# Three chunks of attention ahead of the first MoE, weight pieces spread over 44 units, and z turned in 32x32 squares on VectorE, in a fused attention and two-MoE kernel

## Chip, cores and metric

One core of a Trainium2 chip. The metric is the device time of one execution in microseconds. Three runs of the kernel before gave 5212.89, 5213.58 and 5214.27 us; the median, 5213.58 us, is the time before.

## What is computed

Eight sequences of 3072 tokens pass through attention with a squared ReLU, a gated MLP ("the first MoE") and a mixture of eight experts with one expert a token ("the second MoE"). Cut to what matters:

```python
scores = (1.0 / S) * np.matmul(z, z.transpose(0, 2, 1))      # z: 8 x 3072 x 64
x = u * np.matmul(np.maximum(scores, 0.0) ** 2, v)           # u, v: 8 x 3072 x 256
xn = x / np.sqrt(np.mean(x * x, -1, keepdims=True) + 1e-06) * rms_g
g = xn @ w_gate                                              # 256 x 1536, float64 in memory
x = (g / (1 + np.exp(-g)) * (xn @ w_val)) @ w_out
e_idx, keep = np.argmax(x @ moe2_w_gate, 1), x @ moe2_w_skip > 0
out = x + keep * prob[e_idx] * (np.maximum(x @ w1[e_idx], 0) @ w2[e_idx])
```

## The kernel before

The 24,576 tokens are 48 chunks of 512 (`CH`), six to a sequence. An attention phase of one chunk ("a") and a first-MoE phase of one chunk ("m") have 12 units each. Each fp32 operand is split into a rounded high part and the remainder (`split`, L221 to L228), and one product is three matmuls (`mm3`, L230 to L233). So an attention unit has 4 score matmuls (L566, L567) and 12 on v (L231 to L233), and a MoE unit 12 on gate and value weights and 6 on the output weights, all over 512 columns.

The order is written out by hand. `Stream.unit` issues a unit's front (scores, ReLU and square on ScalarE, the splits on ScalarE, VectorE and GpSimd), and two units later its back, the product that needs the splits (`LAG = 2`). `st.later(d, fn)` puts other steps in front of the unit d units on; every engine's queue, SyncE's DMA issues among them, runs strictly in that order. The phases stand as a0 a1 m0 a2 m1 a3 ... a47 m46 m47, then the second MoE.

Beside the first phases, the first MoE's weights are prepared in 18 pieces (`w_prep`, unit numbers in the table `w_at`). They arrive as float64, and each piece is decoded in three VectorE instructions (`high`, L358 to L360), three more and an addition on GpSimd (`low`, L363 to L371), and split on ScalarE and GpSimd (`parts`, L375, L376). A piece's room is loaded again (`w_next`) when `low` is done with it. In the same stretch eight DMAs of 1325 KB fill the expert buffer with pads (`pad_prep`, L209), one a unit, and `row_prep` (L194 to L198) loads the router's rows.

z is loaded in rows, split on VectorE (`z_split`), put side by side as high and low, turned on TensorE by four 128x128 transposes a chunk (`z_turn`, L269), and copied by ScalarE (L273). For sequence 0 that happens at the start; for the others in the last attention phase before and the MoE phase after it (`batch_prep`).

After a phase come the chunk's tails: attention's product with u and its norm, either through TensorE transposes (`attn_turn`, `xn_turn`, chunks 0, 1 and 47) or in 32x32 squares on VectorE (`in_blocks`), and the MoE's router. The router takes dot products on VectorE (L654) from a copy through memory, or, for the last `QUICK = 2` chunks, transposes (L406) and small matmuls (L637) on TensorE.

Of the kernel before, what the change touches and what calls it, by code (L numbers as in the profile page):

```python
# [20 lines left out]
P = 128  # L21
# [49 lines left out]
def tile_relu2_attention_moe_moe2(  # L71
# [68 lines left out]
    stage = {}  # L140
    for q, tag in ((0, "acct"), (1, "u")):
        g0, g1 = 4 * q, min(NCB, 4 * q + 4)
        if g0 < g1:
            t = sp.tile([P, g1 - g0, KT, DQ], F32, tag=tag, name=f"z0_{q}", bufs=1)
            for g in range(g0, g1):
                nc.sync.dma_start(
                    t[:, g - g0], z[0, g * CH : (g + 1) * CH, :].rearrange("(k p) d -> p k d", k=KT)
                )
                stage["z", 0, g] = t[:, g - g0]

# [63 lines left out]

    st = Stream()
    QUICK = 2
    W_LOW, W_PARTS = 1, 3
    XNT, RS = 3, 2
# [35 lines left out]
    def z_load(b, g):  # L254
        t = sp.tile([P, KT, DQ], F32, tag="z2", name=f"zn_{b}_{g}", bufs=2)
        nc.sync.dma_start(t, z[b, g * CH : (g + 1) * CH, :].rearrange("(k p) d -> p k d", k=KT))
        stage["z", b, g] = t

    def z_split(b, g):
        t = stage.pop(("z", b, g))  # L260
        cat = sp.tile([P, KT, 2, DQ], F32R, tag="zcat", name=f"zc_{b}_{g}", bufs=1)
        split(cat[:, :, 0, :], cat[:, :, 1, :], t)
        stage["zc", b, g] = cat

    def z_turn(b, g):
        cat = stage.pop(("zc", b, g))
        ps = side(f"zps_{b}_{g}")
        for k in range(KT):
            nc.tensor.transpose(  # L269
                ps.bitcast(F32R)[:, 0, k * P : (k + 1) * P], cat[:, k, :, :].rearrange("p a d -> p (a d)"), identr  # L270
            )
# [11 lines left out]
    def v_load(b, g):  # L283
        t = sp.tile([P, KT, D], F32, tag="x" if b == 0 and g % 2 else "stage", name=f"vn_{b}_{g}", bufs=1)
        nc.sync.dma_start(t, v[b, g * CH : (g + 1) * CH, :].rearrange("(k p) d -> p k d", k=KT))
        stage["v", b, g] = t
# [9 lines left out]
    WIDE = moe_w_gate.dtype != F32  # L296
    pieces = [(kind, q, h) for q in range(FQ) for kind in "gv" for h in range(DH)]
    GV = len(pieces)
    pieces += [("o", q, h) for q in range(FQ) for h in range(DH)]

# [8 lines left out]
    def w_room(i):  # L309

        if i < GV:
            return i % 4
        return 0 if i == GV else 4

    def w_load(i):
        kind, q, h = pieces[i]
        w = {"g": moe_w_gate, "v": moe_w_val, "o": moe_w_out}[kind]
        src = w_piece(w, kind, q, h)
        room, n = w_room(i), src.shape[2]
        if room % 4 == 0:  # L320
            tag = "stage" if room else "xn"
            t = sp.tile([P, 2, n], U32 if WIDE else F32, tag=tag, name=f"wst_{i}", bufs=1)
        else:
            t = wraw[:, room - 1, : 2 * n].rearrange("p (o f) -> p o f", o=2)
            t = t if WIDE else t.bitcast(F32)
        nc.sync.dma_start(t, src)
        stage["w", i] = t
# [7 lines left out]
    def w_prep(i):  # L335
# [3 lines left out]
        if kind == "o":  # L339
            f = q * KT + h * KT // 2  # L340
            if i == GV:
                new_wo()
# [6 lines left out]
        if WIDE:  # L349
            bits = t.rearrange("p o (f t) -> p (o f) t", t=2)  # L350
            lo, hi = bits[:, :, 0], bits[:, :, 1]
            flat = (wrb if i < GV and i % 4 > 1 else ytok).rearrange("p k w -> p (k w)")
            dst = flat[:, (i % 2) * CH : (i % 2 + 1) * CH]
# [8 lines left out]
        def low():  # L362
# [7 lines left out]
            )  # L370
            nc.gpsimd.tensor_add(dst, dst, hf)  # L371
            w_next(i)

        def parts():
            nc.scalar.copy(w[:, 0], t)  # L375
            nc.gpsimd.tensor_sub(w[:, 1], t, w[:, 0].bitcast(F32))  # L376
            if not WIDE:
                w_next(i)

        if WIDE:  # L380
            high()
# [48 lines left out]
    def x_blocks(ci, x):  # L430
# [7 lines left out]
        def times_u():  # L438
# [28 lines left out]
    def attn_turn(ci, acct):  # L467
# [61 lines left out]
    def xn_split(ci, t, xn, h):  # L529
# [5 lines left out]
        if h == DH - 1:  # L535
            XN[ci] = xn
            u_load(ci + 1)

    def xn_turn(ci, x):
# [8 lines left out]
        tag, bufs = ("vhl", 6) if ci == NCH - 1 else ("xn", 1)  # L548
        xn = sp.tile([P, 2, DH, CH], F32R, tag=tag, name=f"xn_{ci}", bufs=bufs)
# [3 lines left out]
    def attn_phase(ci):  # L553
# [291 lines left out]
    class Group:  # L845
# [84 lines left out]
        def tail1(self, t, yt):  # L930
# [146 lines left out]
    st.later(2 * NCB - 2, lambda: w_load(GV + 1))  # L1077
    for i, n in enumerate(w_at):
# [3 lines left out]
    for ci in range(NCH):  # L1082
        order.append(("a", ci))
        if ci >= 1:
            order.append(("m", ci - 1))
    order.append(("m", NCH - 1))

    for i, (kind, ci) in enumerate(order):
# [6 lines left out]
        if kind == "a":  # L1095
            if (ci + 1) % NCB == 0 and ci + 1 < NCH:
# [82 lines left out]
```

## Time and profile before

| | |
|---|---|
| median of three runs | 5213.58 us |
| profiled execution, and its span | 5214.61 us, 5212.8 us |
| TensorE (PE) busy | 5132.3 us, 98% |
| VectorE (DVE) busy | 3576.1 us, 69% |
| ScalarE (ACT) busy | 2705.3 us, 52% |
| GpSimd (POOL) busy | 427.3 us, 8% |
| granted TensorE clock, mean | 0.995 |

The span runs from the first to the last instruction; 1.8 us of the execution lie around it. A busy PE is a PE with a matmul in flight: matmuls overlap, so the number of matmuls in a stretch tells more than its busy time.

### The profile page before, as it was taken

What the parts mean: (1) busy time and instruction counts of PE and PEld (TensorE: products, weight loads), DVE (VectorE), ACT (ScalarE), POOL (GpSimd) and SP (SyncE); (2) the same over time, 40 slices, a digit from 0 to 9 for tenths busy, and PEclk for the clock granted to TensorE, in tenths of its full rate; (3) what the DMA queues carried; (4) which work ended last, traced back from release to release, by engine and by line L of the source; (5) the groups of instructions that cost most, each with busy time, mean ns of one, the idle gap of its engine ahead of it and who ended that gap; (6) DMA issues with size and microseconds to landing.
All of it is one profiled execution on the core that took longest, in us unless ns stands there. A gap on an engine that the chain in (4) does not pass through costs nothing. (4 is left out here: it accounts for less than half of the span.)

```text
span 5212.8 us, 65890 instructions
## 1 busy us (share of the span) xinstructions
PE 5132.3 (98%) x23724; PEld 4258.5 (82%) x23724; DVE 3576.1 (69%) x8966; ACT 2705.3 (52%) x3559; POOL 427.3 (8%) x428
## 2 busy tenths in 40 slices
PE   7899999999999999999999999999999999999998
PEld 5688888888888888888888888888888888888888
DVE  8667767677677776777767767777677767554446
ACT  6445545465465554655546546455465554433344
POOL 5100000000000000000000000000000000021111
PEclk9999999999999999999999999999999999999999
DMA  5201101021011110110102001111011110122225
GB/s 163 57 19 42 44 20 37 19 60 26 19 37 35 39 31 19 42 44 20 35 19 66 21 19 37 38 39 27 19 43 43 24 32 19 41 86 86 78 94 161
DMA packets 547841, 234.43 MB, mean 45 GB/s; under 512 B 422357, under 2 KB 528000, under 8 KB 547384
## 3 DMA queue, kind: packets, MB, share of 16 engines
q1 hardware_dynamic: 533496, 205.00, 16.0%
q0 software_dynamic: 14016, 25.21, 1.4%
q8 instruction: 186, 3.05, 0.3%
q14 instruction: 143, 1.17, 0.1%
HBM read 144.79 MB, written 99.30 MB: 47 GB/s over the span
## 5 line engine op out<-in xcount | busy, mean ns | idle before, releaser
L738 ACT ACTIVATE gr<-gv 128x512 f32<-128x512 f32 x576 | 345.9, 600 | 1166.7 <-PE gv L233 1166.7
L232 PE MATMUL acc<-a,v 128*128 128x512 f32 x2304 | 900.3, 391 | 12.7 <-DVE a L228 8.8
L231 PE MATMUL acc<-a,v 128*128 128x512 f32 x2304 | 899.1, 390 | 1.7 <-ACT acct L427 1.7
L233 PE MATMUL acc<-a,v 128*128 128x512 f32 x2304 | 898.9, 390 | 0.0
L228 DVE TENSOR_TENSOR a<-r,a 128x512 fp32r<-128x512 f32 x1128 | 738.5, 695 | 23.4 <-ACT a L227 4.0
L569 ACT ACTIVATE r<-s 128x1024 f32<-128x1024 f32 x576 | 591.3, 1027 | 296.8 <-PE s L567 278.2
L654 DVE CUSTOM_DVE_ANT_0 jk<-ytok,wrb 128x256 bf16<-128x256 f32 x1656 | 698.6, 422 | 35.2
L739 DVE TENSOR_TENSOR gr<-gr,gv 128x512 f32<-128x512 f32 x576 | 395.4, 686 | 442.9 <-ACT gr L738 439.1
L228 DVE TENSOR_TENSOR h<-gr,h 128x512 fp32r<-128x512 f32 x576 | 399.4, 693 | 395.8 <-ACT h L227 395.8
L227 ACT CAST h<-gr 128x512 fp32r<-128x512 f32 x576 | 357.9, 621 | 577.1 <-DVE gr L739 577.1
L570 ACT ACTIVATE r<-r 128x1024 f32<-128x1024 f32 x576 | 611.3, 1061 | 18.4
L703 POOL DMA_INDIRECT xs<-ytok,pu x192 | 210.2, 1095 | 4070.5 <-DVE pu L701 2871.0
L232 PEld LDWEIGHTS acc<-a,v 128*128 128x128 f32 x2304 | 434.0, 188 | 108.3 <-DVE a L228 11.9
L231 PEld LDWEIGHTS acc<-a,v 128*128 128x128 f32 x2304 | 434.4, 189 | 93.2 <-ACT acct L427 2.1
L233 PEld LDWEIGHTS acc<-a,v 128*128 128x128 f32 x2304 | 434.0, 188 | 90.0
L225 DVE CAST a<-r 128x512 fp32r<-128x512 f32 x564 | 237.5, 421 | 340.2 <-ACT r L570 340.0
L231 PE MATMUL gv<-xn,wg_s 128*128 128x512 f32 x1152 | 455.2, 395 | 13.7 <-DVE gr L739 13.6
L567 PE MATMUL s<-z,z 128*128 128x512 f32 x1152 | 452.4, 393 | 0.1
L232 PE MATMUL gv<-xn,wg_s 128*128 128x512 f32 x1152 | 449.4, 390 | 1.1 <-DVE xn L228 1.1
L233 PE MATMUL yacc<-h,wo_s 128*128 128x512 f32 x1152 | 449.4, 390 | 0.6 <-POOL wo_s L376 0.6
L231 PE MATMUL yacc<-h,wo_s 128*128 128x512 f32 x1152 | 449.3, 390 | 0.4 <-ACT wo_s L375 0.4
L232 PE MATMUL yacc<-h,wo_s 128*128 128x512 f32 x1152 | 449.0, 390 | 0.0
(200 smaller groups left out, 9034.4 us busy)
## 6 DMA issues: line engine op xcount, KB each, us to landing
raw<-in_moe_w_dram SPq DMA_DIRECT2D x76, 512.0 KB
vn<-in_v_dram SPq DMA_DIRECT2D x48, 512.0 KB
out_dram<-ytok SPq DMA_DIRECT2D x48, 512.0 KB
ys<-yb SPq DMA_DIRECT2D x368, 64.0 KB
ytok<-ys SPq DMA_DIRECT2D x46, 512.0 KB
u<-in_u_dram SPq DMA_DIRECT2D x360, 64.0 KB
xs<-pad SPq DMA_DIRECT2D x8, 1325.0 KB
xt<-xs SPq DMA_DIRECT2D x16, 530.0 KB
```

The source lines that it names most:

```text
L225: nc.vector.tensor_copy(hi, src)
L227: nc.scalar.copy(hi, src)
L228: (nc.vector if lo_eng == "v" else nc.gpsimd).tensor_sub(lo, src, hi.bitcast(F32))
L231: nc.tensor.matmul(ps, w_hi, x_hi, start=start, stop=False)
L232: nc.tensor.matmul(ps, w_hi, x_lo, start=False, stop=False)
L233: nc.tensor.matmul(ps, w_lo, x_hi, start=False, stop=stop)
L567: nc.tensor.matmul(ps[:, t], zj, zi2, start=False, stop=True)
L569: nc.scalar.activation(out=r, in_=ps, func=AF.Relu)
L570: nc.scalar.activation(out=r, in_=r, func=AF.Square)
L654: nc.vector.tensor_tensor_reduce(out=junk, in0=ytok[:, k, :D], in1=wrb[:, e, :], op0=ALU.mult, op1=ALU.add, scale=1.0, scalar=0.0, accum_o ...
L738: nc.scalar.activation(out=r[:, 0], in_=ps[:, 0], func=AF.Silu)
L739: nc.vector.tensor_mul(r[:, 1], r[:, 0], ps[:, 1])
```

## The change

The new order is a0 a1 a2 m0 a3 m1 ... a47 m45 m46 m47 (`LEAD = 2`), with two x tiles instead of one. The weight pieces go over units 3 to 43 (before: 2 to 33) in another order, with other rooms; their addition and their last subtraction move from GpSimd to VectorE, as does the low part of the second half of a score tile (`split`'s "g"). Pads are asked for every fourth unit from unit 14 (before: every unit from 16), `row_prep` at unit 49 (before: 24). z is loaded in 32-token by 32-feature squares, twice (so that both halves of the partitions hold the features), turned by one VectorE transpose, and split there; PE and ACT take no part in it. `QUICK` is 3.

```diff
+    def z_in(t, b, g):
+        blocks = z[b, g * CH : (g + 1) * CH, :].rearrange("(b c) (q r) -> q c b r", c=Q, r=Q)
+        for q in range(4):
+            nc.sync.dma_start(t[q * Q : (q + 1) * Q].rearrange("p (b r) -> p b r", r=Q), blocks[q % 2])
+        stage["z", b, g] = t
...
-            st.later(first + e, fill)
+            st.later(first + 4 * e, fill)
...
-    QUICK = 2
-    W_LOW, W_PARTS = 1, 3
+    LEAD = 2
+    QUICK = 3
+    W_LOW, W_PARTS = 1, 2
...
     def z_split(b, g):
-        t = stage.pop(("z", b, g))
-        cat = sp.tile([P, KT, 2, DQ], F32R, tag="zcat", name=f"zc_{b}_{g}", bufs=1)
-        split(cat[:, :, 0, :], cat[:, :, 1, :], t)
+        t = sp.tile([P, CH], F32, tag="zcat", name=f"zt_{b}_{g}", bufs=1)
+        nc.vector.transpose(t, stage.pop(("z", b, g)))
...
     def z_turn(b, g):
-        for k in range(KT):
-            nc.tensor.transpose(
-                ps.bitcast(F32R)[:, 0, k * P : (k + 1) * P], cat[:, k, :, :].rearrange("p a d -> p (a d)"), identr
-            )
         z1 = sp.tile([P, CH], F32R, tag="z1", name=f"z1_{b}_{g}", bufs=NCB)
-        nc.scalar.copy(z1, ps[:, 0, :])
+        nc.vector.tensor_copy(z1, t)
+        nc.vector.tensor_sub(z1[DQ:, :], t[DQ:, :], z1.bitcast(F32)[DQ:, :])
...
-            nc.gpsimd.tensor_add(dst, dst, hf)
+            nc.vector.tensor_add(dst, dst, hf)
             w_next(i)
-        def parts():
+        def high_part():
             nc.scalar.copy(w[:, 0], t)
-            nc.gpsimd.tensor_sub(w[:, 1], t, w[:, 0].bitcast(F32))
+        def low_part():
+            nc.vector.tensor_sub(w[:, 1], t, w[:, 0].bitcast(F32))
...
-        return 2 <= ci < NCH - 1
+        return LEAD < ci < NCH - 1
...
-                    split(o[:, 0], o[:, 1], r[:, t], "a" if t == 1 or ci == 1 else "v", "g" if t == 1 and ci <= 1 else "v")
+                    split(o[:, 0], o[:, 1], r[:, t], "a" if t == 1 or (0 < ci <= LEAD and k % 2) else "v")
...
-    st.later(2 * UPC, row_prep)
-    pad_prep(4 * UPC // 3)
+    st.later(4 * UPC + 1, row_prep)
+    pad_prep(UPC + 2)
...
-    w_at = [2, 4, 6, 8, 10, 11, 13, 14, 15, 16, 18, 19, 20, 21, 24, 27, 30, 33]
+    w_at = [3, 7, 11, 13, 15, 18, 21, 24, 27, 29, 31, 33, 35, 37, 38, 39, 41, 43]
...
-        if ci >= 1:
-            order.append(("m", ci - 1))
-    order.append(("m", NCH - 1))
+        if ci >= LEAD:
+            order.append(("m", ci - LEAD))
+    order += [("m", ci) for ci in range(NCH - LEAD, NCH)]
```

The order on DVE in chunk 0, from the low step of the first weight piece to unit 6 (`wst` is the piece as loaded, `ytok` its decoding, `a` a split score tile, `zc` and `zt` z before it is turned and after). Before:

```order
L363 SCALAR_TENSOR_TENSOR ytok<-wst_168,ytok 128x512
L366 TENSOR_SCALAR wst_168<-ytok 128x512
L368 SCALAR_TENSOR_TENSOR wst_168<-wst_168 128x512
L225 CAST a_3_0_274<-r_3_271 128x512
L228 TENSOR_TENSOR a_3_0_274<-r_3_271,a_3_0_274 128x512
L225 CAST zc_3_292<-z_0_78 128x4x64
L228 TENSOR_TENSOR zc_3_292<-z_0_78,zc_3_292 128x4x64
```

And now:

```order
L376 SCALAR_TENSOR_TENSOR ytok<-wst_180,ytok 128x512
L379 TENSOR_SCALAR wst_180<-ytok 128x512
L381 SCALAR_TENSOR_TENSOR wst_180<-wst_180 128x512
L384 TENSOR_TENSOR ytok<-ytok,wst_180 128x512
L234 CAST a_4_0_305<-r_4_302 128x512
L237 TENSOR_TENSOR a_4_0_305<-r_4_302,a_4_0_305 128x512
L237 TENSOR_TENSOR a_4_1_308<-r_4_302,a_4_1_308 128x512
L276 CAST z_0_3_324<-zt_3_289 128x512
L277 TENSOR_TENSOR z_0_3_324<-zt_3_289,z_0_3_324 64x512
L237 TENSOR_TENSOR v_3_327<-vn_3_207,v_3_327 128x1024
```

The piece's addition, the second low part and z's split have joined DVE's queue; GpSimd's queue, which held such rows throughout these phases, holds none of them now.

The order on PE where a sequence begins, in its first attention phase. Before:

```order
L233 MATMUL acc_4578<-a_0_1_4617,v_0_4196 128x512
L269 MATMUL zps_4_4687<-ident,zc_4_4626 128x128 x4
L566 MATMUL s_3_4701<-z_1_0_4099,z_1_1_4260 128x512
L567 MATMUL s_3_4701<-z_1_0_4223,z_1_1_4260 128x512
L566 MATMUL s_3_4701<-z_1_0_4099,z_1_1_4260 128x512
```

And now:

```order
L242 MATMUL acc_4161<-a_0_1_4200,v_0_3787 128x512
L586 MATMUL s_3_4281<-z_1_0_3684,z_1_1_3846 128x512
L587 MATMUL s_3_4281<-z_1_0_3814,z_1_1_3846 128x512
L586 MATMUL s_3_4281<-z_1_0_3684,z_1_1_3846 128x512
L587 MATMUL s_3_4281<-z_1_0_3814,z_1_1_3846 128x512
```

The 48 rows of z transposes are gone from PE.

The order on SyncE (SP) around the pads (`wst`, `wraw` and, after the change, `wrb` are rooms of weight pieces; what an issue waits for stands behind it). Before:

```order
L326 DMA wst_758<-in_moe_w_out_dram 128x2x512 [waits DMAHW7_49,Pool_49]
L209 DMA xs<-pad 128x10x265 [waits DMAHW6_49]
L209 DMA xs<-pad 128x10x265
L209 DMA xs<-pad 128x10x265 [waits DMAHW0_49]
L209 DMA xs<-pad 128x10x265 [waits DMAHW1_49]
L209 DMA xs<-pad 128x10x265 [waits DMAHW2_49]
L209 DMA xs<-pad 128x10x265 [waits DMAHW3_49]
L326 DMA wst_999<-in_moe_w_out_dram 128x2x512 [waits DMAHW4_49,Pool_49]
```

And now:

```order
L339 DMA wrb<-in_moe_w_out_dram 128x2x512 [waits DMAHW4_49]
L216 DMA xs<-pad 128x10x265
L216 DMA xs<-pad 128x10x265 [waits DMAHW6_49]
L216 DMA xs<-pad 128x10x265 [waits DMAHW7_49]
L417 DMA u_1061<-in_u_dram 128x4x256 [waits DMAHW3_49,DMAHW0_49,DVE_49]
L339 DMA wst_1100<-in_moe_w_gate_dram 128x1024 [waits DMAHW1_49,DVE_49]
L216 DMA xs<-pad 128x10x265 [waits DMAHW2_49]
L339 DMA wst_1174<-in_moe_w_gate_dram 128x1024 [waits DVE_49]
```

Six pads stood in a row between two weight loads; now at most three do, and the rest stand one by one.

## Rows read from the trace of the kernel before

**Rows 1.** The page: busy time, share and instructions of each engine.

```profile
PE 5132.3 (98%) x23724; PEld 4258.5 (82%) x23724; DVE 3576.1 (69%) x8966; ACT 2705.3 (52%) x3559; POOL 427.3 (8%) x428
```

**Rows 2.** Windows: stretch, length, busy and count by engine, PE clock, DMA share, GB/s.

```profile
0.00:253.05 253.05, 202.43 (x825) 158.18 (x825) 191.92 (x310) 145.48 (x198) 92.17 (x81) 0.93 0.42 114
...
100.00:150.00 50.00, 38.23 (x150) 28.37 (x149) 43.93 (x63) 29.18 (x39) 30.58 (x21) 0.93 0.76 220
150.00:200.00 50.00, 36.23 (x151) 29.24 (x150) 23.91 (x43) 14.15 (x29) 7.49 (x6) 0.83 0.43 69
...
305.24:439.53 134.29, 134.22 (x592) 110.60 (x593) 97.07 (x256) 83.16 (x102) 8.60 (x10) 1.00 0.17 36
```

**Rows 3.** Timeline of PE: a unit of a0, the first of m1 (start us, us).

```profile
13.37 0.80 PE L566 MATMUL s<-z,z 128*128 128x512 f32 x1
...
253.05 0.39 PE L231 MATMUL gv<-xn,wg_s 128*128 128x512 f32 x1
```

**Rows 4.** Waits of PE, 0 to 253 us (total us, times, longest us).

```profile
PE gv L231 <- DVE gr L739: 13.6, 1, 13.6
PE zps L269 <- DVE zc L228: 13.4, 5, 3.9
```

**Rows 5.** Timeline: DVE beside GpSimd, then alone (in brackets: idle before).

```profile
17.00 1.62 POOL L228 TENSOR_TENSOR a<-r,a 128x512 fp32r<-128x512 f32 x1 [2.50 <-ACT a L227]
17.38 1.40 DVE L225 CAST zc<-z 128x256 fp32r<-128x256 f32 x1
...
175.29 0.43 DVE L358 TENSOR_SCALAR ytok<-wst 128x512 uint32<-128x512 uint32 x1 [17.24 <-DMA wst<-in_moe_w_out_dram]
175.75 0.43 DVE L359 TENSOR_SCALAR ytok<-ytok 128x512 f32<-128x512 f32 x1
```

**Rows 6.** Timeline of SP: the pads, the router's rows and a weight piece.

```profile
103.25 20.04 SPq L209 DMA_DIRECT2D xs<-pad  x6
...
147.81 6.55 SPq L197 DMA_DIRECT2D wsc<-in_moe_w_skip_dram  x1
167.28 0.35 SPq L198 DMA_DIRECT2D wrb<-wsc  x1
167.74 0.38 SPq L326 DMA_DIRECT2D wst<-in_moe_w_out_dram  x1
```

**Rows 7.** Groups over the span: count, busy us, mean ns, idle before.

```profile
L228 DVE TENSOR_TENSOR a<-r,a 128x512 fp32r<-128x512 f32 x1128 | 738.5, 695 | 23.4 <-ACT a L227 4.0
L225 DVE CAST a<-r 128x512 fp32r<-128x512 f32 x564 | 237.5, 421 | 340.2 <-ACT r L570 340.0
L228 DVE TENSOR_TENSOR v<-vn,v 128x1024 fp32r<-128x1024 f32 x48 | 58.8, 1226 | 13.3 <-ACT v L227 13.3
L411 DVE STREAM_TRANSPOSE xt<-x 128x1024 f32<-128x1024 f32 x45 | 55.7, 1239 | 0.0
L570 ACT ACTIVATE r<-r 128x1024 f32<-128x1024 f32 x576 | 611.3, 1061 | 18.4
```

**Rows 8.** Window of three phases where a sequence begins; PE at one transpose (timeline).

```profile
491.74:629.97 138.23, 137.01 (x617) 112.45 (x617) 107.63 (x274) 91.43 (x114) 8.62 (x10) 1.00 0.26 63
...
596.49 0.53 PE L269 MATMUL zps<-ident,zc 128*128 128x128 f32 x4 [1.17 <-DVE yb L411]
```

**Rows 9.** Timeline of PE in the router step of chunk 46.

```profile
4549.87 1.04 PE L406 MATMUL yps<-ident,yt 128*128 128x128 f32 x8
4553.25 3.59 PE L637 MATMUL lps<-wrt,yt 128*128 128x9 f32 x16 [2.34 <-DVE gr L739]
4556.69 0.77 PE L231 MATMUL yacc<-h,wo_s 128*128 128x512 f32 x1
```

**Rows 10.** Timeline: first z loads and their user; eight loads in 32x32 squares.

```profile
0.81 3.20 SPq L146 DMA_DIRECT2D z<-in_z_dram  x6
3.09 0.29 DVE L225 CAST zc<-z 128x256 fp32r<-128x256 f32 x1 [1.46 <-DMA z<-in_z_dram]
...
177.80 4.05 SPq L397 DMA_DIRECT2D u<-in_u_dram  x8
```

More of the change, by code (lines that the diff above doesn't have):

```diff
@@ L140, in tile_relu2_attention_moe_moe2, with z_first @@
     stage = {}
[L141 to L147, printed above, removed]
-                )
-                stage["z", 0, g] = t[:, g - g0]
+    wrb = cpool.tile([P, E + 1, D], F32, name="wrb")
+    def z_in(t, b, g):
[3 more added lines that the diff above has]
+        stage["z", b, g] = t
+    z0 = [sp.tile([P, 2 * CH], F32, tag=tag, name=f"z0_{tag}", bufs=1) for tag in ("acct", "u")]
+    z0.append(wrb.rearrange("p k w -> p (k w)")[:, 2 * CH : 4 * CH])
+    assert NCB == 6
+    def z_first(g):
+        z_in(z0[g // 2][:, g % 2 * CH : (g % 2 + 1) * CH], 0, g)
+    z_first(0)
     eye = sp.tile([P, P], F32, tag="vhl", name="eye", bufs=6)
@@ L283, in v_load @@
     def v_load(b, g):
-        t = sp.tile([P, KT, D], F32, tag="x" if b == 0 and g % 2 else "stage", name=f"vn_{b}_{g}", bufs=1)
+        t = sp.tile([P, KT, D], F32, tag="x" if b == 0 and g % 2 else "stage", name=f"vn_{b}_{g}", bufs=2 if b == 0 and g % 2 else 1)
         nc.sync.dma_start(t, v[b, g * CH : (g + 1) * CH, :].rearrange("(k p) d -> p k d", k=KT))
@@ L296, in tile_relu2_attention_moe_moe2, with gv_pieces @@
     WIDE = moe_w_gate.dtype != F32
-    pieces = [(kind, q, h) for q in range(FQ) for kind in "gv" for h in range(DH)]
+    def gv_pieces(q):
+        return [(kind, q, h) for kind in "gv" for h in range(DH)]
+    pieces = gv_pieces(0) + gv_pieces(1)
     GV = len(pieces)
-    pieces += [("o", q, h) for q in range(FQ) for h in range(DH)]
+    pieces += [("o", 0, 0), ("o", 0, 1), ("o", 1, 0)] + gv_pieces(2) + [("o", 1, 1), ("o", 2, 0), ("o", 2, 1)]
+    assert FQ == 3
     def w_piece(w, kind, q, h):
@@ L319, in w_load @@
         room, n = w_room(i), src.shape[2]
-        if room % 4 == 0:
-            tag = "stage" if room else "xn"
-            t = sp.tile([P, 2, n], U32 if WIDE else F32, tag=tag, name=f"wst_{i}", bufs=1)
-        else:
-            t = wraw[:, room - 1, : 2 * n].rearrange("p (o f) -> p o f", o=2)
+        dt = U32 if WIDE else F32
+        if room in (0, 4):
+            t = sp.tile([P, 2, n], dt, tag="stage" if room else "xn", name=f"wst_{i}", bufs=1)
+        elif room == 5:
+            t = wp.tile([P, 2, n], dt, tag="wst", name=f"wst_{i}")
+        else:
+            if room == 6:
+                t = wrb.rearrange("p k w -> p (k w)").bitcast(U32)[:, 2 * CH : 2 * CH + 2 * n]
+            else:
+                t = wraw[:, room - 1, : 2 * n]
+            t = t.rearrange("p (o f) -> p o f", o=2)
             t = t if WIDE else t.bitcast(F32)
@@ L340, in w_prep @@
             f = q * KT + h * KT // 2
-            if i == GV:
+            if not wo:
                 new_wo()
@@ L351, in w_prep @@
             lo, hi = bits[:, :, 0], bits[:, :, 1]
-            flat = (wrb if i < GV and i % 4 > 1 else ytok).rearrange("p k w -> p (k w)")
+            flat = (wrb if i % 4 > 1 else ytok).rearrange("p k w -> p (k w)")
             dst = flat[:, (i % 2) * CH : (i % 2 + 1) * CH]
@@ L416, in in_blocks @@
     def in_blocks(ci):
-        return 2 <= ci < NCH - 1
+        return LEAD < ci < NCH - 1
     def attn_tail0(ci, acc):
         if in_blocks(ci):
-            x = sp.tile([P, DH, NB, Q], F32, tag="x", name=f"x_{ci}", bufs=1)
+            x = sp.tile([P, DH, NB, Q], F32, tag="x", name=f"x_{ci}", bufs=2)
             turn_blocks(x, acc)
@@ L472, in attn_turn @@
         )
-        x = sp.tile([P, KT, D], F32, tag="x", name=f"x_{ci}", bufs=1)
+        x = sp.tile([P, KT, D], F32, tag="x", name=f"x_{ci}", bufs=2)
         attn_tail1(ci, acct, pv, x)
@@ L522, in xn_prep @@
             turn_blocks(t, x)
-            xn = sp.tile([P, 2, DH, CH], F32R, tag="xn", name=f"xn_{ci}", bufs=1)
+            tag, bufs = xn_room(ci)
+            xn = sp.tile([P, 2, DH, CH], F32R, tag=tag, name=f"xn_{ci}", bufs=bufs)
             for h in range(DH):
@@ L939, in tail1 @@
             tag = "stage" if self.outs[0] == 1 else ("u", "x")[self.outs[0] % 2]
-            ot = sp.tile([P, n, D], F32, tag=tag, name=f"ot_{self.i}_{t}", bufs=1)
+            ot = sp.tile([P, n, D], F32, tag=tag, name=f"ot_{self.i}_{t}", bufs=1 + (tag == "x"))
             for k in range(n):
@@ L1054, in tile_relu2_attention_moe_moe2 @@
     v_split(0, 0)
+    z_first(3)
     v_load(0, 2)
+    z_first(4)
+    z_first(5)
     st.later(2 * NCB - 3, lambda: u_load(0))
```

57 lines of the change are left out of this document (27 added, 30 removed).

## The prediction

> **What bounds the kernel now.** The page comes first: PE has a matmul in flight for 98% of the span [rows 1], so only three things can shorten it: fewer PE instructions, fewer gaps, or less time at the lower clock. The windows then tell where PE is slow. Inside a sequence, two attention phases and a MoE phase hold 588 wide matmuls (180, 228 and 180) in 134.29 us [rows 2], or 0.228 us each with their small extras. That is the pace to compare with; it makes an attention unit 3.65 us and a MoE unit 4.11 us. Up to 253.05, where m1 begins [rows 3], PE has done 36 attention units and 12 MoE units less the backs of two units, 36x16 + 12x18 - 24 = 768 matmuls, worth 175.4 us. So 77.6 us are lost there, and almost nothing inside a sequence. The waits of PE name 13.6 us for DVE in the first MoE and 13.4 us for z on DVE [rows 4]; the rest is shorter waits and a granted clock of 0.93 over the stretch, down to 0.83 from 150 to 200 us [rows 2], that is, times at 1.2 instead of 2.4 GHz around the gaps.
>
> Behind PE's waits stands DVE, busy for 191.9 of the first 253 us [rows 2]. Part of that is not work: a 128x256 cast took 1.40 us while a GpSimd subtraction ran, whereas a 128x512 instruction alone took 0.43, with 0.46 from one to the next [rows 5]. GpSimd was busy for 92 us there [rows 2]. The gap of 13.6 us has another root: DVE stood 17.24 us for a weight piece [rows 5] whose load SP issued at 167.74, right behind the router's `wrb`, which had waited for a write issued at 147.81; the pads had kept SP for 20 us before that [rows 6]. One load in a strict queue stopped DVE, then ScalarE and PE.
>
> **The change, part by part.** *First phases.* The same point is now the start of a3: 36 attention units and 12 MoE units less two MoE backs, 780 matmuls or 178.2 us at the steady pace. To that come the losses.
>
> Fill: before, the third unit starts at 13.37 [rows 3]. Now z's first chunk takes four issues of about 0.5 us (eight took 4.05 us [rows 10]) and lands 1.8 us after the last one (before, one issue of some 0.5 us from 0.81, its user at 3.09 [rows 10]): 4.7 us instead of 3.1. The turn and two splits on DVE stand in for a path over DVE, PE, ACT that they shorten, so I take 13.7 us. Eight matmuls (1.8 us) are done by then: 11.9 us lost.
>
> DVE's pace: I price its queue from the order, with 0.03 us added to each duration for the pitch [rows 5]. The low-part subtraction is 0.72 us, the cast 0.45, a v split 1.26 [rows 7]. A weight piece is 4 instructions of 0.46 and 4 of 0.72, 4.75 us; I take its decoding of two operands at the subtraction's price. A z turn is half a 128x1024 transpose (1.24 us [rows 7]), 0.65, and its split 1.17. A score tile's splits are 1.90 a unit, 1.45 where ScalarE casts both halves.
> - Units 0 to 8: nine splits 17.1, five v 6.3, five z splits and four turns 8.5, the pieces' steps 8.8, a z swap 0.9: 41.5 against 32.9 us of PE, +8.6.
> - a1 and a2: splits 40.2, pieces 47.5 (nine whole, two in part), the tails of chunks 0 and 1 some 11: 98.7 against 87.6 and 3 of transposes, +8.
> - The first nine units of m0: pieces 26.4, products and splits of the MoE 13, the tail of chunk 2 and a z swap 7: 46.3 against 37.0, +9.3.
>
> Together 25.9 us. From a unit's front to the back that needs it, two units on, there are about 3 us more than the chain scores, ReLU, square (1.06 us [rows 7]), splits needs, so each of the three dense stretches may hide 3 us: low end 16. If every unit above PE's pace stalls and no thin one makes up for it, the excesses sum to 42: high end. ScalarE, which now casts both halves in every second unit of a1 and a2, adds a little; I take 27, near the low sum, since dense and thin units alternate. GpSimd's 92 us leave with nothing to pay: no row of its tensor instructions is left in this stretch of the order, and DVE's slowed ones [rows 5] come down to their prices above.
>
> PE transposes of the tails by then (chunks 0 to 2 and one normalised x, 32 at 0.11 us, by the pitch of such transposes, eight in 1.04 us with the last one's 0.27 in it [rows 9]): 3.5 us. Loss 11.9 + 27 + 3.5 = 42.4, so a3 starts at 220.6. Before, that work was done at 253.05 + 12x0.228 = 255.8. **Gain 35.2 us.** Before, the turns of normalised x of chunks 0 and 1 both lay inside the 253 us; now those of chunks 1 and 2 come after a3's start: 16 more, **+1.8 us**.
>
> The late piece: all weight loads now stand ahead of the router's rows on SP, and pads at most three in a row (the order): six issues held SP for 20 us [rows 6], eight in the queue kept the DMA share at 0.76 [rows 2]. SP is paced by its waits alone, so "every fourth unit" is not what happens; but the three adjacent pads go out around unit 16 and no load behind them is wanted before unit 33. The router's rows go out early too, around unit 40: from 147.81 to 167.28 is 20 us [rows 6], and DVE's first use of them is in unit 54. I cost them at nothing; without this lead a3 would wait some 10 us.
>
> *z.* Where a sequence begins, the same three phases take 138.23 us [rows 8] against 134.29 [rows 2]: 3.94 us for six z turns on PE and one 1.17 us wait [rows 8]. All of that leaves PE, for seven sequences: **-27.6 us**. DVE pays 6 x (0.65 + 1.17 - 0.8) = 6 us a sequence in a stretch where it is busy 107.6 of 138 us [rows 8], which hides it. The load goes from one issue to four, twice the bytes: 2.05 us of issue plus 1.8 of landing, 3.9 us [rows 10], against a lead of two units or more, 7 us; hidden too.
>
> The rows show 128-byte pieces leaving at the pace of SP's issues, eight DMAs in 4.05 us [rows 10]. The Trainium skill (DMA: Bandwidth & Descriptors, Specifications) says that a transfer wants 512 bytes to reach line rate and that smaller ones cost a read-modify-write, which speaks against this change. By the rows the sum stays; by that rule, with landing three times as slow as I take it, it stays as well, since 7.5 us just exceed the lead and meet the slack of 3.
>
> *Router steps.* Chunk 45 now takes PE's path: eight transposes 0.9, sixteen small matmuls 3.44 (4553.25 to 4556.69 [rows 9]), **+4.3 us**. Chunk 46 also waited 2.34 there and then ran at the lower clock, 8.2 us in all, for a weight load that nothing of the kind has in m46; that is the high end.
>
> **Sum.** The profiled execution took 5214.6 us (span 5212.8 and 1.8 around). 5214.6 - 35.2 + 1.8 - 27.6 + 4.3 = 5157.9; the median before is 1.0 below that execution: 5157 us.
>
> **Rivals.**
> - *DVE is the bound of the whole start.* All excesses stall (42) and clock dips add 5: 20 us less gain, 5177. For it: DVE was 88% busy from 100 to 150 us [rows 2], and every dense stretch is above PE's pace. Against: GpSimd's interference is gone. Chance 0.17.
> - *The dense units hide.* Stalls of 11 instead of 27: 5141. For it: phases inside a sequence run DVE at 72% (97.07 of 134.29 us) with PE idle for 0.07 us [rows 2]. Chance 0.12.
> - *z moves its wait to DVE.* The seven sequences give nothing back, because DVE stands for its loads where PE stood: 5185. For it: the last z load of a sequence is released by the transpose ten DVE rows ahead of its own. Chance 0.06.
> - *Slower than before.* DVE's queue is strict, and 42 z chunks now stop it until their squares land. It decides when loading outlasts the lead of 7.3 us and the slack of 3: each us beyond costs 42. To end 0.2% above before, 57 + 10 us must be eaten, 1.6 a chunk, so a landing some 10 us after the last issue. The rows show 1.8 for rows of z; no row shows the landing of the squares. 5225 or more; chance 0.04.
>
> That the change doesn't do what it says holds for the pads alone, at no price.
>
> **Numbers.** My case (5146 to 5170) has 0.61. The range goes from the hidden case's 5139 to 5186, which takes in the worst DVE pace, the high router price and the lost z gain one at a time. A measurement here tells 0.2%, 10 us, from no change. Faster 0.94, same 0.02, slower 0.04.
>
> **What would show it.** Right: a3 starts near 220 us, no GpSimd tensor work before it, no wait over 5 us in m0; phases with a new sequence as long as the others (134.3 us for three); PE still 98% or more busy; a router step in m46 of some 4 to 5 us. Wrong: DVE with idle time ended by z or weight loads, PE gaps at its z scores, or a3 beyond 240 us.

## The result and the profile after

The changed kernel takes **5168.41 us** (median of 4 runs, 5167.55 to 5169.0); the kernel before took 5213.93 us beside it (4 runs, 5212.89 to 5215.59). The ratio is 0.9915 with a 95% interval of 0.9903 to 0.9927: 45.5 us or 0.9% faster. The forecast was 5157, so the time lies 11 us above it and inside its range. The profiled execution's span fell from 5212.8 to 5165.8 us, by 47.0, and that is what the sums below go by.

The engines' line of the page after the change:

```profile
PE 5104.3 (99%) x23570; PEld 4238.6 (82%) x23570; DVE 3593.6 (70%) x9002; ACT 2678.2 (52%) x3521; POOL 347.5 (7%) x368
```

Against [rows 1], PE has 154 matmuls fewer and 28.0 us less to do, POOL 60 instructions and 80 us less. PE's busy time alone doesn't give 47 us; the rest is gaps. The windows after the change, in the order start to a3, a1, a2, m0, then the three phases where a sequence begins (a5, m3, a6), m3 alone, and the last MoE phases m46 and m47:

```profile
0.00:213.06 213.06, 191.09 (x813) 153.48 (x813) 179.88 (x349) 142.92 (x198) 3.91 (x21) 0.98 0.52 134
...
59.10:104.50 45.40, 44.72 (x202) 36.79 (x200) 39.79 (x76) 40.16 (x56) 0.00 (x0) 1.00 0.63 178
104.50:152.44 47.94, 46.22 (x210) 37.54 (x208) 42.70 (x89) 38.58 (x55) 0.00 (x0) 1.00 0.34 101
152.44:213.06 60.62, 55.56 (x238) 44.38 (x236) 49.25 (x100) 23.91 (x44) 0.14 (x1) 0.97 0.54 109
...
401.10:539.02 137.92, 134.95 (x592) 110.50 (x593) 113.13 (x280) 87.49 (x108) 9.52 (x10) 1.00 0.31 69
442.13:497.85 55.72, 52.75 (x233) 42.88 (x232) 43.45 (x108) 18.15 (x30) 0.00 (x0) 1.00 0.21 54
...
4436.67:4489.50 52.83, 52.83 (x251) 44.06 (x251) 24.86 (x66) 17.74 (x28) 8.05 (x9) 1.00 0.14 50
4489.50:4542.24 52.74, 52.74 (x252) 43.95 (x250) 24.26 (x45) 21.32 (x31) 14.12 (x9) 1.00 0.14 45
```

Three things are to be seen. The start is shorter than forecast, with POOL empty. The three phases of a new sequence take 137.92 us, hardly less than the 138.23 of [rows 8]: PE does the 592 matmuls of an ordinary stretch [rows 2], not 617, and still loses the same time. And the last phases run without a gap.

The waits of PE up to a3, and the places on PE's timeline that the forecast named:

```profile
PE s L586 <- DVE z L277: 14.4, 5, 6.7
PE gv L240 <- DVE gr L759: 5.1, 4, 2.7
```

```profile
15.24 0.77 PE L586 MATMUL s<-z,z 128*128 128x512 f32 x1 [4.33 <-DVE z L277]
...
213.06 0.39 PE L586 MATMUL s<-z,z 128*128 128x512 f32 x1
...
491.60 0.50 PE L240 MATMUL gv<-xn,wg_s 128*128 128x512 f32 x1 [1.05 <-DVE gr L759]
...
497.85 0.50 PE L586 MATMUL s<-z 128*128 128x512 f32 x1 [1.78 <-DVE gr L759]
```

a3 starts at 213.06, not 220.6. The 13.6 us for the gate product in m0 [rows 4] have become 5.1 us in four waits. The last two rows are new: waits of 1.05 and 1.78 us at the end of m3. They come again in each of the seven sequences: over the whole span PE waits seven times, 12.4 us in all, for such scores behind VectorE's `gr`.

**The sum by its terms** (us, before to after):

| Term | forecast | measured |
|---|---|---|
| start of a3, against 255.8 before | -35.2 | -42.7 |
| turns of normalised x in a3 and a4 | +1.8 | +1.6 (41.72 and 41.91 against 41.04) |
| z, seven sequences | -27.6 | 7 x (137.92 - 138.23) = -2.2 |
| last router steps | +4.3 | -3.5 |
| sum | -56.7 | -46.8, of a span that fell by 47.0 |

For the last term: m45, m46, m47 took 52.20 + 53.80 + 58.70 = 164.7 us before and take 158.4 now; 2.7 of that difference are the 12 matmuls that the new order has already done at a3's start, which the first term counts. So one term hit, one was nearly all lost, and two came out better. The experiments ask why.

### The profile page after: what moved, and what is told of

It is laid out like the page before. It is cut to its first block, busy times and chain, and to the rows that moved or that the text cites. A ratio compares the mean times of both kernels' runs of the same rounds, so it can differ in the third digit from the quotient of the medians.

```text
span 5165.8 us, 65678 instructions
## 1 busy us (share of the span) xinstructions
PE 5104.3 (99%) x23570; PEld 4238.6 (82%) x23570; DVE 3593.6 (70%) x9002; ACT 2678.2 (52%) x3521; POOL 347.5 (7%) x368
## 5 line engine op out<-in xcount | busy, mean ns | idle before, releaser
L674 DVE CUSTOM_DVE_ANT_0 jk<-ytok,wrb 128x256 bf16<-128x256 f32 x1620 | 683.3, 422 | 34.4
L240 PE MATMUL gv<-xn,wg_s 128*128 128x512 f32 x1152 | 454.5, 395 | 13.5 <-DVE gr L759 12.5
L242 PE MATMUL gv<-xn,wg_s 128*128 128x512 f32 x1152 | 449.0, 390 | 0.0
L241 PE MATMUL gv<-xn,wg_s 128*128 128x512 f32 x1152 | 449.0, 390 | 0.0
L242 PE MATMUL yacc<-h,wo_s 128*128 128x512 f32 x1152 | 448.6, 389 | 0.0
L240 PE MATMUL gv<-xn,wv_s 128*128 128x512 f32 x1152 | 448.5, 389 | 0.0
```

The lines of the kernel that those rows point to most:

```text
L240: nc.tensor.matmul(ps, w_hi, x_hi, start=start, stop=False)
L241: nc.tensor.matmul(ps, w_hi, x_lo, start=False, stop=False)
L242: nc.tensor.matmul(ps, w_lo, x_hi, start=False, stop=stop)
L674: nc.vector.tensor_tensor_reduce(out=junk, in0=ytok[:, k, :D], in1=wrb[:, e, :], op0=ALU.mult, op1=ALU.add, scale=1.0, scalar=0.0, accum_o ...
```

## Experiments

Each ran beside the kernel before on the same chip, whose median lay between 5212.5 and 5213.9 us. Line numbers in rows are those of the kernel that ran; in an experiment with added lines they are shifted.

### Where z's 27.6 us went

VectorE's timeline at the end of m3 in the changed kernel:

```profile
487.72 1.23 DVE L237 TENSOR_TENSOR v<-vn,v 128x1024 fp32r<-128x1024 f32 x1 [0.26 <-ACT v L236]
...
490.86 0.68 DVE L759 TENSOR_TENSOR gr<-gr,gv 128x512 f32<-128x512 f32 x1
492.23 0.69 DVE L237 TENSOR_TENSOR h<-gr,h 128x512 fp32r<-128x512 f32 x1 [0.69 <-ACT h L236]
492.84 0.42 DVE L276 CAST z<-zt 128x512 fp32r<-128x512 f32 x1
493.29 0.69 DVE L277 TENSOR_TENSOR z<-zt,z 64x512 fp32r<-64x512 f32 x1
493.99 1.23 DVE L473 TENSOR_TENSOR x<-x,rstdb 128x1024 f32<-128x1024 f32 x1
495.14 0.68 DVE L759 TENSOR_TENSOR gr<-gr,gv 128x512 f32<-128x512 f32 x1
```

The gate products (`gr`) at 490.86 and 495.14 stand behind v's split, eight short instructions of a router step and three of x's scale (left out, 488.86 to 490.94), z's split and the scaling of x, and PE waits for each of them. What VectorE itself waits for in m3 and a6:

```profile
DVE h L237 <- ACT h L236: 8.2, 12, 0.7
```

No idle time there ends with a load. But in each of the 12 units it stands 0.69 us until ScalarE has cast the gate product, and nothing behind that place in its queue can be done meanwhile.

**e3, z back on PE.** `z_load`, `z_split` and `z_turn` take the lines of the kernel before for every sequence but the first:

```
     def z_turn(b, g):
+        if b:
+            cat = stage.pop(("zc", b, g))
+            ps = side(f"zps_{b}_{g}")
...
+            nc.scalar.copy(z1, ps[:, 0, :])
+            Z1[b, g] = z1
+            return
         t = stage.pop(("zt", b, g))
```

> Edit: z of sequences 1 to 7 goes as in the kernel before (rows loaded by one DMA, split on VectorE, four PE transposes, ScalarE's copy); sequence 0 and everything else stays as in the changed kernel. It undoes one part. Theory A (the change swapped some 3.9 us of PE's turns for 3.5 us of waits behind VectorE): the three phases with a new sequence take 138.2 us instead of 137.9, 5168 to 5172. If the forecast's own term were right (27.6 us came back and were lost elsewhere): 5190 or more. Rival D (turning z on VectorE costs more than PE's turns did): 5160 or less.

5167.89 us (5166.4 to 5169.36), the changed kernel's time. The window of the three phases and PE's wait in it:

```profile
399.50:537.75 138.25, 137.03 (x616) 112.44 (x617) 107.52 (x274) 91.43 (x114) 9.61 (x10) 1.00 0.26 63
```

```profile
PE zps L284 <- DVE yb L445: 1.2, 1, 1.2
```

Theory A holds: with z on PE the stretch is 138.25 us, with z on DVE 137.92. The change traded PE's turns and one wait for waits behind VectorE's queue. PE has 24 transposes fewer to do in this stretch, and no time is won by it.

**e1, z's splits later; e2, v's last two as well; e5, v's chunk 3 too; e10, v early.** All four change z's units in `batch_prep`:

```
-            st.later((3, 5, 10, 15, 17)[g - 1], lambda g=g: z_turn(b, g))
+            st.later((3, 7, 12, 15, 17)[g - 1], lambda g=g: z_turn(b, g))
```

e2, e5 and e10 change v's as well; here e10's, the others' in the table below:

```
-            st.later((1, 4, 6, 8, 11, 16)[g], lambda g=g: vt(g), mid=True)
+            st.later((0, 1, 4, 6, 13, 17)[g], lambda g=g: vt(g), mid=True)
```

> Edit: in the MoE phase before a new sequence, the splits of z's turned chunks 2 and 3 on VectorE go two units later (units 7 and 12 instead of 5 and 10). Theory A (the 3.5 us that m3 is longer than other MoE phases, 55.72 against 52.20 us, come from VectorE's strict queue being late in units 6, 10 and 11 of it): each z split is 1.15 us of that queue, so the waits of 0.14 us at 473.88 and some 1.1 of the 2.8 us at 491.60 and 497.85 go; m3 near 54.3, 7 sequences x 1.3 = 9 us, 5159 (5156 to 5163). Theory B (VectorE has too much work over the whole start of a sequence, so that what leaves one unit stalls another): 5168 within 3, with waits of the same sum at other units. Theory C (the squares of z land late): 5168, and VectorE's idle time before its 32x32 transposes ends with a DMA of z.

> Edit: as the run before, and the low-part splits of v's chunks 4 and 5 go from units 11 and 16 to 13 and 17. Theory A: the gate product of units 10 and 11 is no longer behind 1.48 us of v and 1.15 of z; m3 comes down to 52.2 to 52.8, 7 x 3 = 21 us, 5147 (5144 to 5152). Theory B: the first attention phase of the sequence grows by what m3 loses: 5165 to 5171. Theory C: 5168.

> Edit: as e2, and v's chunk 3 is split at unit 11 instead of 8, chunks 4 and 5 at 14 and 18. In e2 m3 still took 54.54 us; VectorE's row there shows v's split of 1.22 us at 487.42 ahead of the 2.4 us of a router step and the gate product at 490.56. Theory A (a full strict queue in units 9 to 11 of the MoE phase): m3 comes to 52.2 to 53, 7 x 1.5 to 2.3 us less than e2's 5157, so 5141 to 5147. Theory B (too much work over the whole start): no more than 2 us below e2, with waits in the first attention phase instead. Had z's move alone been the cause, v's split would be without effect: 5157.

> Edit: the changed kernel with the z splits of e2 (units 3, 7, 12, 15, 17) and v's chunks 0 to 5 split at units 0, 1, 4, 6, 13, 17 (changed kernel: 1, 4, 6, 8, 11, 16), so that none of v falls into units 8 to 12, where router step, x scale and z stand. Theory A (the strict queue of the last third of the MoE phase is full, while its first two units leave VectorE 3.9 us idle): m3 52.2 to 53 and a6 41.0, the phases with a new sequence near 134.5 us, 5141 to 5147. Theory B (total work): what m3 gains comes back as waits in m3's first units or in a6, 5154 or more.

| | v's units | us | the three phases | m3 | a6 |
|---|---|---|---|---|---|
| changed kernel | 1, 4, 6, 8, 11, 16 | 5168.41 | 137.92 | 55.72 | 41.17 |
| e1 | 1, 4, 6, 8, 11, 16 | 5164.7 (5164.17 to 5165.45) | 137.60 | 54.50 | 42.00 |
| e2 | 1, 4, 6, 8, 13, 17 | 5157.19 (5155.81 to 5157.92) | 136.60 | 54.54 | 41.02 |
| e5 | 1, 4, 6, 11, 14, 18 | 5154.76 (5153.5 to 5155.29) | 136.10 | 53.07 | 42.04 |
| e10 | 0, 1, 4, 6, 13, 17 | 5151.04 (5150.1 to 5152.33) | 135.64 | 53.61 | 41.03 |

e10's window of the three phases and the end of its m3 on VectorE:

```profile
400.90:536.54 135.64, 134.84 (x592) 110.40 (x593) 112.86 (x280) 87.43 (x108) 9.55 (x10) 1.00 0.32 70
```

```profile
491.05 0.69 DVE L237 TENSOR_TENSOR h<-gr,h 128x512 fp32r<-128x512 f32 x1 [0.69 <-ACT h L236]
491.66 1.22 DVE L473 TENSOR_TENSOR x<-x,rstdb 128x1024 f32<-128x1024 f32 x1
492.80 0.68 DVE L759 TENSOR_TENSOR gr<-gr,gv 128x512 f32<-128x512 f32 x1
```

VectorE's work in the three phases is the same, 112.9 us against 113.1; only its order differs, and 17 us of the kernel's time are gone (ratio to the kernel before 0.9881, interval 0.9865 to 0.9898). That rules out theory B as the whole cause, and C, since z's loads are where they were. But each size that theory A gave was too large, and none of the four runs came inside the range it gave for the time. In e1 the 1.2 us that m3 won came back in a6 as 0.8, which is what B said. In e2 m3 didn't move, since v's chunk 3 still stood ahead of the router step. In e5 that chunk, moved to m3's last unit, made a6 1.0 us longer: its split of 1.23 us now stands in VectorE's queue ahead of a6's first score split, which began 5.57 us after a6's start (4.08 in e10). e10 put two of v's splits into the first two units, where PE works on long attention backs and VectorE had stood idle for up to 2.0 us at a time in the changed kernel. Of 3.6 us a sequence, 1.35 remain; what would take them away was not tried.

**e12, z on PE with e10's units.** e3's edit and e10's two tables together, in short:

```
     def z_turn(b, g):
+        if b:
...
+            st.later((3, 7, 12, 15, 17)[g - 1], lambda g=g: z_turn(b, g))
+            st.later((0, 1, 4, 6, 13, 17)[g], lambda g=g: vt(g), mid=True)
```

> Edit: as e10 (v split at units 0, 1, 4, 6, 13, 17, z at 3, 7, 12, 15, 17), but z of sequences 1 to 7 goes the old way over PE, as in e3. The question: is z by squares on VectorE worth anything once v's splits are out of the way? Theory P (yes: PE's six turns of z and the wait for VectorE's long transposes, 1.16 us in e3, stay, and only VectorE's own waits could be healed by v's move; e3's three phases took 138.25 us, e10's 135.7): 137 to 138.3 us for the three phases, 5160 to 5168. Rival Q (no: v's splits were the whole wait, and the old way is as good): 5147 to 5154.

5218.7 us (5213.76 to 5222.27): both theories fell. PE's longest wait from 213 to 560 us, and ScalarE's timeline ahead of it:

```profile
PE ssps L486 <- ACT z L288: 3.0, 1, 3.0
```

```profile
475.73 0.62 ACT L236 CAST h<-gr 128x512 fp32r<-128x512 f32 x1 [1.67 <-DVE gr L776]
476.25 1.04 ACT L236 CAST v<-vn 128x1024 fp32r<-128x1024 f32 x1
477.20 0.58 ACT L288 CAST z<-zps 128x512 fp32r<-128x512 f32 x1
```

The units that suit z on VectorE don't suit it on PE: a turn at unit 7 holds PE's spare result tile (in PSUM) until ScalarE has copied it out, that copy stands behind a cast that waits for VectorE and behind v's, and PE's sum for x (`ssps`) wants the same tile. The window a5, m3, a6 was 145.80 us. So this run says what a turn in an unsuitable unit costs, and leaves open how the old way with units of its own would do beside e10. An estimate: in e3 PE waits only 1.2 us in that stretch, so without any wait it would take some 137.1 us, still 1.4 above e10's.

### What shortened the start

**e7, the router's rows later, in the kernel before.**

```
-    st.later(2 * UPC, row_prep)
+    st.later(3 * UPC, row_prep)
```

> Edit: one line of the kernel before: the router's rows (wsc, wrb) are asked for at unit 36 instead of 24, behind all weight pieces; all else is the kernel before. Theory I (the wait of 13.6 us for the gate product came from the weight load that stood behind wrb in SP's queue): that wait goes, 8 to 13 us less, 5201 to 5206. Rival J (VectorE's own work would have been late there anyway): a wait of over 8 us stays at that place, 5209 to 5214.

5196.72 us (5196.06 to 5198.27; ratio 0.9969, 0.9957 to 0.998): 16.7 us from one line. m0 in the kernel before, then in e7:

```profile
138.00:209.80 71.80, 56.48 (x238) 45.29 (x238) 38.34 (x62) 25.27 (x45) 16.94 (x13) 0.88 0.39 73
```

```profile
137.90:193.03 55.13, 53.39 (x237) 43.39 (x236) 39.02 (x62) 25.19 (x45) 16.89 (x13) 1.00 0.35 73
```

Theory I holds, and more than its upper end came: the wait of 13.6 us is gone, and the granted clock of m0 rose from 0.88 to 1.00, which goes with the other 3 us.

**e6, GpSimd back, in the changed kernel.**

```
-            nc.vector.tensor_add(dst, dst, hf)
+            nc.gpsimd.tensor_add(dst, dst, hf)
...
-            nc.vector.tensor_sub(w[:, 1], t, w[:, 0].bitcast(F32))
+            nc.gpsimd.tensor_sub(w[:, 1], t, w[:, 0].bitcast(F32))
...
-                    split(o[:, 0], o[:, 1], r[:, t], "a" if t == 1 or (0 < ci <= LEAD and k % 2) else "v")
+                    split(o[:, 0], o[:, 1], r[:, t], "a" if t == 1 or (0 < ci <= LEAD and k % 2) else "v", "g" if t == 1 and ci <= 1 else "v")
```

> Edit: in the changed kernel the weight pieces' additions and low parts go back to GpSimd, and so do the low parts of every second score tile of a0 and a1; everything else stays. Theory G (the start gains from VectorE being free of GpSimd's neighbourhood, although VectorE does 43 us more itself): a1, a2 and m0 grow by 10 to 25 us together, 5178 to 5194. Rival H (the order alone, three phases ahead and pieces over 44 units, makes the start; VectorE's lighter queue offsets the interference): 5160 to 5172.

5183.53 us (5181.22 to 5184.38), 15.1 slower than the changed kernel. e6's window up to a3, with two of VectorE's groups up to 225 us; then the same groups of the changed kernel:

```profile
0.00:225.84 225.84, 193.83 (x813) 154.49 (x813) 192.23 (x289) 142.84 (x198) 93.85 (x81) 0.98 0.50 126
```

```profile
L237 DVE TENSOR_TENSOR a<-r,a 128x512 fp32r<-128x512 f32 x48 | 45.8, 975 | 4.9 <-PE acc L242 2.9 <-ACT a L236 1.2
...
L372 DVE TENSOR_SCALAR ytok<-ytok 128x512 f32<-128x512 f32 x10 | 8.2, 816 | 0.3
```

```profile
L237 DVE TENSOR_TENSOR a<-r,a 128x512 fp32r<-128x512 f32 x78 | 50.5, 689 | 5.4 <-ACT a L236 4.4
...
L372 DVE TENSOR_SCALAR ytok<-ytok 128x512 f32<-128x512 f32 x10 | 4.3, 427 | 0.3
```

Theory G holds in kind, though the three phases it named, a1, a2 and m0, grew by 8.8 us and not by 10 or more: a0, a1 and a2 grew by 4.0, 5.1 and 5.1 us, and m0 shrank by 1.4. VectorE has 60 instructions fewer, 289 for 349, and is busy longer, 192.2 us for 179.9 in a shorter stretch: the same clamp takes 816 ns on average with GpSimd at work and 427 without. Work given to GpSimd cost VectorE more here than doing it.

**e4, z's second chunk first.** At the start `z_turn(0, 1)` follows its load directly.

```
     z_split(0, 1)
+    z_turn(0, 1)
     v_split(0, 0)
```

> Edit: at the start, VectorE turns and splits z's second chunk right after its load instead of behind v's split, the constants and the first unit's splits. Theory E (the gap of 4.33 us before the third unit's scores is this order alone): the z split ends near 11.7 instead of 15.10, the third unit starts near 11.9, 2 to 3.4 us gained, 5165 to 5166.5. Rival F (the first unit's own splits and v's split come 1.15 us later and hold up the backs): the gap moves to the first back, 5167 to 5169.

5168.96 us (5168.1 to 5170.21): no change, rival F. The third unit's scores now start at 11.29, and PE waits at the first back instead, e4's timeline:

```profile
11.29 0.47 PE L586 MATMUL s<-z,z 128*128 128x512 f32 x1 [0.36 <-DVE z L277]
...
13.48 0.51 PE L240 MATMUL acc<-a,v 128*128 128x512 f32 x1 [1.02 <-DVE a L234]
```

The whole of a0 took 52.5 us in both. VectorE is busy for 46.1 of the 52.4 us in the changed kernel, which suggests that it is the bound there and that this edit only chose the place of the wait; the granted clock of a0 was also lower in e4, 0.94 against 0.97.

**e11, the weight pieces a unit or two earlier, on top of e10.**

```
-    w_at = [3, 7, 11, 13, 15, 18, 21, 24, 27, 29, 31, 33, 35, 37, 38, 39, 41, 43]
+    w_at = [3, 7, 10, 12, 14, 17, 20, 22, 25, 27, 29, 31, 33, 35, 37, 38, 40, 42]
```

> Edit: as e10, and the weight pieces after the second are prepared one or two units earlier (3, 7, 10, 12, 14, 17, 20, 22, 25, 27, 29, 31, 33, 35, 37, 38, 40, 42). Theory O (m0's waits, 2.67, 1.51 and 0.71 us for the gate product, come from the last five pieces, 4.75 us of VectorE each, standing among m0's own products; a1 and a2 still have room): 2 to 4 us below e10, m0 below 59. Rival B (the whole start is full): m0's waits move to a1 and a2, within 1.5 us of e10.

5153.94 us (5152.89 to 5155.37), 2.9 above e10: a3 starts at 214.47 instead of 212.80. e11's waits of PE up to a3:

```profile
PE gv L240 <- DVE gr L759: 4.6, 3, 2.8
PE acc L240 <- ACT acct L444: 3.5, 2, 2.8
```

m0 was 1.0 us shorter, a2 2.6 longer. Theory O fell. Rival B has the kind right, the waits moved to a2, but not the size, since the run lies further above e10 than its 1.5 us.

### The end

Theory for the gain at the end: in the kernel before, the first expert's weights came late. GpSimd's last scatter of chunk 45, the loads behind it on SP, and ScalarE's cast that waited, in the kernel before; then SP and ScalarE after the change:

```profile
4542.12 0.97 POOL L703 DMA_INDIRECT xs<-ytok,pu  x1 [1.58 <-DMA xs<-ytok,pu]
...
4544.44 0.83 SPq L898 DMA_DIRECT2D xt<-xs  x2
...
4550.93 1.04 ACT L227 CAST w<-raw 128x1024 fp32r<-128x1024 f32 x1 [7.00 <-DMA raw<-in_moe_w_dram]
```

```profile
4482.15 0.83 SPq L918 DMA_DIRECT2D xt<-xs  x2
...
4502.52 1.05 ACT L236 CAST w<-raw 128x1024 fp32r<-128x1024 f32 x1
```

**e8, two buffers of x in the kernel before**, at each use of the tag "x"; one of them:

```
-            x = sp.tile([P, DH, NB, Q], F32, tag="x", name=f"x_{ci}", bufs=1)
+            x = sp.tile([P, DH, NB, Q], F32, tag="x", name=f"x_{ci}", bufs=2)
```

> Edit: in the kernel before, the tile x gets two buffers instead of one, as the changed kernel has; all else is the kernel before. Theory K (at the end, ScalarE stood 7 us for an expert's raw weights, whose load SP issued behind a load that waited for x's buffer): m47 falls from 58.7 us to 53 to 55, 5208 to 5211. Rival L (it is the order of the last chunks, not the buffer): m47 stays, 5213.

5214.47 us (5212.11 to 5216.01; ratio 1.0002, 0.9992 to 1.0012). ScalarE's wait in m47 of e8:

```profile
ACT w L227 <- DMA raw<-in_moe_w_dram: 7.7, 2, 7.1
```

The wait is as long as before; theory K fell. m47 was 57.20 instead of 58.70, without effect on the whole.

**e9, QUICK = 3 in the kernel before.**

```
-    QUICK = 2
+    QUICK = 3
```

> Edit: one number of the kernel before, QUICK = 3 instead of 2: chunk 45's router step goes over PE as well; one buffer of x, the old order and all else stay. Theory M (at the end of the kernel before, the first expert's raw weights stand in SP's queue behind token loads that wait for chunk 45's scatters, which GpSimd issued from 4534 to 4543 us; done earlier, the weights are there when ScalarE wants them): m47 falls from 58.7 us to 53 to 54, the step itself costs 3 to 4 us in a47 or m46, together 1 to 3 us less, 5210 to 5212. Rival N (the price of 4.3 us and nothing back): m47 stays at 58.7, 5217.

5210.51 us (5209.57 to 5211.59; ratio 0.9995, 0.9986 to 1.0005): the time alone is within what can be told from no change; the trace decides. Windows of a47 and m47 in e9, and SP's token loads:

```profile
4435.38:4479.31 43.93, 43.89 (x206) 36.41 (x207) 26.83 (x65) 35.51 (x41) 8.27 (x9) 1.00 0.10 36
...
4532.82:4585.58 52.76, 52.76 (x251) 43.96 (x250) 24.23 (x45) 21.27 (x31) 13.77 (x9) 1.00 0.14 45
```

```profile
4497.06 19.97 SPq L898 DMA_DIRECT2D xt<-xs  x2
```

Theory M holds: m47 falls from 58.70 to 52.76, and chunk 45's step costs 2.8 us in a47 (43.93 against 41.10). With its scatters done a phase earlier, the tokens and the weights behind them leave SP before m47.

## Why the forecast was right, and where it was not

- **The start** was right in kind and 7.5 us too small. The fill was taken as 11.9 us; with the third unit at 15.24 it is 13.4, because z's split waits behind v's and the first unit's splits. VectorE's pace, the time that PE loses to a VectorE too full, was taken as 27 us. Against the matmuls at 0.228 us and 0.9 for eight transposes, the excess is 7.4 in a0 behind the third unit (forecast 8.6), 3.1 in a1 and a2 (8), 7.7 in m0 (9.3): some 18. The term that was mis-sized is VectorE's work in a1 and a2, priced at 98.7 us. It was busy there for 82.5 and stood another 9.3 for ScalarE; PE alone needs some 90. Splits took 34.5 us for 40.2, weight pieces 42.7 for 47.5, the tails some 5 for 11. The mean durations held, 689 ns for the low part and 427 for the clamp, but the pause added to each did not: two low parts in a row take 1.29 us, not 1.44. So the low end of 16 was closer, though not for its reason, the lead that hides work. No GpSimd work was left, as forecast.
- **The cause of the 13.6 us** was read rightly from SP's queue; e7 shows it by one line. **GpSimd's removal** is worth 12.8 us up to a3 in the new order (e6: 225.84 against 213.06). Both together are 29.5 of 42.7 us if they add up, which no run shows. What the spread pads, the 44 units and three phases ahead give each was not told apart.
- **z** is the step that failed: "in a stretch where it is busy 107.6 of 138 us [rows 8], which hides it". Of its 27.6 us 2.2 came. The load on VectorE was right, 5.5 us more against 6 forecast, but a mean over 138 us says nothing of the units where router step, v, z and x stand in one row ahead of a gate product, with 0.69 us a unit that can't be used. The rival "z moves its wait to DVE" has the outcome, nothing back from seven sequences, with another cause: it blamed the loads. Its second half, 5185, didn't come, since the other terms gave more.
- **z's loads**: SP and VectorE at the very start of the changed kernel:

```profile
0.81 2.00 SPq L147 DMA_DIRECT2D z_acct<-in_z_dram  x4
...
3.38 2.37 SPq L147 DMA_DIRECT2D z_acct<-in_z_dram  x4
...
4.71 0.71 DVE L269 STREAM_TRANSPOSE zt<-z_acct 128x512 f32<-128x512 f32 x1 [3.08 <-DMA z_acct<-in_z_dram]
...
9.86 0.71 DVE L269 STREAM_TRANSPOSE zt<-z_acct 128x512 f32<-128x512 f32 x1 [2.35 <-DMA z_acct<-in_z_dram]
```

  For the first chunk four issues end at 2.81 and the transpose starts at 4.71: 1.9 us, as forecast. The second chunk's issues end at 5.75, with a load of v between the two, and its transpose starts at 9.86, 4.1 us later, after 2.35 of waiting. So the landing was not 1.8 us under load, and the forecast of the fill left that wait out. Those are the only two of 48 such transposes that wait for a load; that disposes of the rival "slower". The Trainium skill (DMA: Bandwidth & Descriptors, Specifications) wants 512 bytes for line rate. Whether the pieces of 128 bytes made the second landing longer, or the traffic beside them, no run tells; the later loads are early enough for either.
- **The router step** of chunk 45 was taken at 4.3 us and costs 2.8 (e9). The row that it was read from [rows 9] stood behind a wait of 2.34 us and ran at a granted clock of 0.50, the lower level: sixteen small matmuls in 3.44 us. In the changed kernel, at 1.00, they take 1.71, from 4456.72 to 4458.43. Missed was what it sets free: the load for which ScalarE stood 7.0 us in m47 waited for chunk 45's scatters. The prediction knew the 8.2 us there and called them a high end; they were a gain.
- **DVE as the bound of the whole start** and **the dense units hide** missed on either side: some 18 us of stalls against 42 and 11, about midway between 11 and the 27 taken.

The forecast came within 11 us because an error of 25 us one way met 7.5 and 7.8 the other way. That is luck: the time lies in the band of the main case, 5146 to 5170, but that case counted on z's gain, so the band doesn't bear it out.

## What to carry to other kernels

Whether VectorE hides an added step is read unit by unit in its queue, ahead of the instruction that PE waits for, with the idle time that a cast on another engine leaves counted as taken; a busy share over a phase is no answer. When work moves between engines, look again at the units of everything beside it: here two tables of numbers, v's units and z's, gave 17 us more than the change (e10), and the same units with z on PE (e12) lost 50 against e3. A load that waits for a late write holds up all that stands behind it on SP, so ask what each moved step lets go earlier.

## What the runs showed of the hardware

VectorE's instructions took longer with GpSimd's elementwise work in the start: 816 ns for 427, 975 for 689 as means (e6). A gap on PE cost more than its length: without the wait of 13.6 us m0 became some 16.5 us shorter (e7). The lower clock behind a gap isn't fixed either. After almost the same wait near 50 us, 2.49 and 2.48 us, the next unit of a0 ran at a mean granted clock of 0.71 in the changed kernel and 1.00 in e5; the windows, the changed kernel first:

```profile
50.33:55.47 5.14, 5.14 (x16) 4.14 (x17) 4.22 (x7) 3.16 (x4) 0.00 (x0) 0.71 0.58 209
```

```profile
50.17:53.90 3.73, 3.73 (x16) 3.08 (x17) 3.70 (x6) 2.91 (x4) 0.00 (x0) 1.00 0.80 291
```

That is 1.4 us, so differences of this size between two starts say nothing.
